# Attention beside an MLP on one core: four numbers of the schedule changed (first load of the output projection, pace of the MLP, split of a weight piece, release of raw weights)

## The chip, the cores and the metric

The kernel runs on one core of a Trainium2 chip. The metric is device time in microseconds (us), from the start to the end of one execution. The core has five engines that each run their own instructions in order: TensorE (PE; its weight loads are shown apart as PEld), VectorE (DVE), ScalarE (ACT), GpSimd (POOL) and SyncE (SP), which here only issues transfers. A line such as L580 is line 580 of the kernel before.

## The reference

All is float32, with 2048 tokens, 576 channels, 32 heads of 18 channels and an MLP with 4608 hidden channels:

```
g = sigmoid((x * gate_w).sum(-1, keepdims=True))
qkv = (x @ wqkv).reshape(1, 2048, 3, 32, 18)
p = softmax(einsum("bhqd,bhkd->bhqk", q, k) * 18 ** -0.5)
a = einsum("bhqk,bhkd->bhqd", p, v) -> (1, 2048, 576) @ wo
b = gelu(layernorm(x) @ w1 + b1) @ w2 + b2
return g * a + (1 - g) * b
```

The softmax is over all 2048 keys, and gelu is the tanh form.

## The kernel before

**Numbers.** To keep float32 accuracy with the matrix engine's rounded format (fp32r), an operand is held as a rounded part (hi) and the rest (lo), and a product is made of three matmuls: hi by hi, hi by lo and lo by hi. A split is thus a copy (hi) and a subtraction (lo).

**Start.** x is transposed on TensorE (L768). The weights wqkv come in seven column pieces, cut by W_CUT; `split_w` makes hi on ScalarE (L762) and lo on VectorE or POOL (L763). Pieces 0 and 1 are split in two parts, the chunks 0 to 2 and the chunks 3 and 4 of the 576 input channels; the later pieces in one. q and k are the matmuls at L892, L894 and L895, v those at L913 to L916. This phase ends at about 228 us.

**Loop.** The attention is a loop of 512 steps: 32 units (a unit is two heads over half of the tokens) by 16 key blocks. In a step TensorE computes scores for the row maxima of a later unit (L229, reduced by VectorE at L231), scores for the exponential (L272, taken by ScalarE at L275), and, every two or three steps (`span`), a burst of products of the probabilities with v (L290). At the end of a unit's maxima VectorE finishes them (L239 to L242), TensorE transposes them (L246), ScalarE copies the rows (L248), and two transfers (L138) put them behind the queries; they go on POOL's queue or on SP's, depending on how long ago the last large load was. The sums and products of a finished unit are copied by VectorE (L301) and stored (L304, L310).

In the gaps between these matmuls the MLP's run: a generator gives them out piece by piece. A hidden tile is 54 matmuls at L492 (`h_pair`), followed by an activation chain on ScalarE (L513, L545, L543) and POOL (L182), which gives the split result hh and hl. An output tile is 48 matmuls at L580 (`out_pair`), added up by VectorE (L597) out of two accumulators. The pieces of a hidden tile are spread over one or two groups of gaps; what decides is how much work has been given out, against a pace:

```
behind[0] = base + (TOTAL - base) * step / FIN
...
elif (last and spent[0] >= behind[0]) or left < GAPS:
    left += GAPS
```

So FIN is the step at which the pace has all the MLP's work done. The MLP's weights are loaded raw and split once (ScalarE L396, POOL L182), stored, and loaded again for later token blocks. `LOADED` holds the slot from which a raw weight may be taken up: LAND (8) slots after its load was issued. Work that isn't TensorE's is queued (`bg`, `defer`) and handed out by slots.

**Output projection.** It is a generator too. `next(proj)` runs its first parts at the steps of PSTEP: at 489 the raw wo is loaded (L1059, L1057) and five splits are queued for POOL (L1052, L1053); at the second number `load_o(0)` and `load_den(0)` load a quarter of the attention's results (L1071, L1074) and its sums (L1096, L1099); at 495 seven stages of `normed(0, c)` are deferred (VectorE L1140 and L1150, ScalarE between) and two finished tiles of the MLP are loaded (L1128); at 497 the next quarter follows. The results are loaded into a tile of the pool that also held the raw wo. When the MLP is done and step 498 is past, the matmuls of the projection (L1227) take the MLP's place in the gaps; those left at the loop's end run behind it. VectorE mixes at L1231, and `out` is stored at L1238 or L1241. The MLP's finished output goes through memory: stored at L604, loaded at L1122.

Of the kernel before, what the change touches and what calls it, by code (L numbers as in the profile page):

```python
# [40 lines left out]
LAND = 8  # L41
# [7 lines left out]
PLAN = [[(), (0,), (1,), (2,), (3,), (4,), (5, 6), ()], [(), (0,), (1,), (2,), (3,), (4,), (5, 6), ()],  # L49
        [(), (), (), (0, 1), (2,), (3,), (4, 5), (6,)]]  # L50
LAST = 28
PSTEP = (489, 492, 495, 497)
ORDER = (0, 1, 3, 2)
ROUNDS = [lambda g: 0, lambda g: 2 * (g in (9, 10, 16)), lambda g: 2 * (g % 2 or g == 16),
          lambda g: 2 * (g in (4, 5, 6, 7, 8, 10, 12, 14))]
# [6 lines left out]
W_AT = {0: 1, 1: 2, 2: 3, 4: 4, 6: 5, 7: 6}  # L62
W_CUT = (0, 128, 416, 704, 992, 2 * D, 3 * D - 288, 3 * D)
NSTEP = 512
FIN = NSTEP - 12
TWOS = NSTEP - 2 * NT


# [1 line left out]
def gated_mix_kernel(ctx: ExitStack, tc: tile.TileContext, x, wqkv, wo, w1, b1, w2, b2, gate_w, out):  # L70
# [70 lines left out]
    slot = [0]  # L141
# [61 lines left out]
    def load_k(pair, c0=0, c1=S):  # L203
        ka = KA[pair % 2]
        for h in range(2):
            d0 = D + (2 * pair + h) * DH
            for i, part in enumerate((0, 1, 0)):
                r = 64 * h + i * DH
                dma_r(nc.sync, ka[r:r + DH, c0:c1], qk_scr[part, d0:d0 + DH, c0:c1])
# [120 lines left out]
    looped = [False]  # L330
# [9 lines left out]
    def mlp():  # L340
# [3 lines left out]
        n = len(seq)  # L344
# [17 lines left out]
        def raw2(c):  # L362
            return R2[min(c // 2, 1)][c % 2]
        LOADED = {}
# [12 lines left out]
        def load_w2(c):  # L377
            if (2, c) in LOADED or c >= NFC:
                return
            LOADED[2, c] = slot[0] + LAND  # L380
            nc.sync.dma_start(raw2(c), w2[c * P:(c + 1) * P, :])

        def rounded(dst, src):
# [47 lines left out]
        def prep_w2(i):  # L431
            for m in range(G // 2):
                q = i * (G // 2) + m
                for j in range(2):
                    c = 2 * (q % NQ0) + j
                    if q >= NQ0:
                        reload(W2, (q, j), wp2, [P, 2, D], w2_scr[c])
                        continue
                    split(W2, (q, j), wp2, [P, 2, D], (2, c), raw2(c), w2_scr[c],
                          lambda c: load_w2(c + 2))  # L440
# [190 lines left out]
        for late, fn, k in ((1, load_w2, 0), (1, load_w2, 1), (3, load_w1, 1), (4, load_w2, 2), (4, load_w2, 3)):  # L631
            defer(late, lambda fn=fn, k=k: fn(k))
# [82 lines left out]
    with ExitStack() as a:  # L715
# [41 lines left out]
        def split_w(n, eng):  # L757
            c0 = W_CUT[n] if W_CUT[n] < 2 * D else W_CUT[n] - 2 * D
            hi, lo = [w_[:, :, c0:c0 + W_CUT[n + 1] - W_CUT[n]] for w_ in (W_QK if W_CUT[n] < 2 * D else W_V)]
            raw = wraw.pop(n)  # L760
            for cs in (slice(0, 3), slice(3, 5)) if n < 2 else (slice(0, 5),):
                nc.scalar.activation(hi[:, cs], raw[:, cs], AF.Copy)  # L762
                eng.tensor_tensor(lo[:, cs], raw[:, cs], hi[:, cs].bitcast(F32), op=ALU.subtract)  # L763

# [178 lines left out]
        for c in range(5):  # L943
            x_chunk(0, c)
            if c == 2:
                split_w(0, nc.vector)
                load_w(2)
        b1r = sm.tile([NFC, P], F32, name="b1r", bufs=1)
        for tb in range(NB):
            work = [(qk_group, (tb, mt)) for mt in (range(9) if tb < 2 else (4, 0, 1, 2, 3, 5, 6, 7, 8))] + [(v_group, (tb, t, n)) for t in range(4) for n in range(2)]  # L950
            for g, (fn, args) in enumerate(work):
                if tb == 0:
                    if g in W_AT:
                        n = W_AT[g]
                        split_w(n, nc.gpsimd if 2 < n < 6 else nc.vector)
                        if n + 2 < 7:
                            load_w(n + 2)
                    if g == 10:
                        nc.sync.dma_start(b2b, bcast_rows(b2, D))
                        nc.sync.dma_start(b1r, b1.rearrange("(c p) -> c p", p=P))  # L960
# [9 lines left out]
                if tb + 1 < NB:  # L970
# [12 lines left out]
                    c = g - at["x"]  # L983
# [267 lines left out]
    def fill(step, gap):  # L1251

        if over[0] is None and not stream and kept[0] == NT and step > PSTEP[-1] + 1:
            stream.append(proj)
            over[0] = step
            spent[0] = since[0] = 0.0
        if over[0] is None:
            piece[0] = gap
            behind[0] = base + (TOTAL - base) * step / FIN
            if gap not in skip:  # L1260
# [17 lines left out]
    for u in range(NU):  # L1278
        for kc in range(NT):
# [10 lines left out]
            if NU - 5 <= u < NU - 3 and kc % 4 == 1 and 0 < step - 16 * (NU - 5) - 1 < 17:  # L1290

                kb = (step - 16 * (NU - 5) - 5) // 4
                load_k(NPAIR - 1, kb * TB, (kb + 1) * TB)
            if step in PSTEP:
                assert hidden[0] == NB - 1
# [51 lines left out]
```

## Time and profile before

| | |
|---|---|
| median of 3 runs | 2227.85 us (2227.79 to 2228.08) |
| the profiled execution | 2229.34 us, span 2227.6 us |
| granted TensorE clock, mean | 1.000 |
| busy: TensorE, weight loads, VectorE, ScalarE, POOL | 99%, 71%, 74%, 64%, 45% of the span |
| TensorE, matmuls: L492 (64 rows, the large group), L580 (hh and hl) | 569.4 us, 487.1 + 351.1 us |
| TensorE: L272, L229 | 460.4 us, 435.1 us |
| transfers | 329.23 MB, mean 148 GB/s |

The profile gives busy time by group of instructions, the waits of each engine with what ended them, and the chain of work that ended last. A timeline row shows start, length, engine, line, instruction and count, and in square brackets the idle time ahead of it with its releaser. A row of the chain shows start, length and the work.

### The profile page before, as it was taken

What the parts mean: (1) busy time and instruction counts of PE and PEld (TensorE: products, weight loads), DVE (VectorE), ACT (ScalarE), POOL (GpSimd) and SP (SyncE); (2) the same over time, 40 slices, a digit from 0 to 9 for tenths busy, and PEclk for the clock granted to TensorE, in tenths of its full rate; (3) what the DMA queues carried; (4) which work ended last, traced back from release to release, by engine and by line L of the source; (5) the groups of instructions that cost most, each with busy time, mean ns of one, the idle gap of its engine ahead of it and who ended that gap; (6) DMA issues with size and microseconds to landing.
All of it is one profiled execution on the core that took longest, in us unless ns stands there. A gap on an engine that the chain in (4) does not pass through costs nothing.

```text
span 2227.6 us, 51540 instructions
## 1 busy us (share of the span) xinstructions
PE 2209.8 (99%) x20528; PEld 1583.7 (71%) x20528; DVE 1648.6 (74%) x2888; ACT 1429.3 (64%) x2655; POOL 1003.5 (45%) x1001
## 2 busy tenths in 40 slices
PE   8999999999999999999999999999999999999999
PEld 7878666766667766777666776766776776777668
DVE  6675777777778778777777777777777777777734
ACT  4333777777776666666666666666665666666772
POOL 4321766666664444444444444444444444444710
PEclk9999999999999999999999999999999999999999
DMA  8867555444464533333354424232464323242264
GB/s 266 270 222 220 192 174 162 145 159 148 151 195 139 195 102 120 123 120 104 113 171 151 136 79 135 100 124 100 120 177 145 107 103 121 102 148 93 89 223 168
DMA packets 164119, 329.23 MB, mean 148 GB/s; under 512 B 56830, under 2 KB 84090, under 8 KB 153150
## 3 DMA queue, kind: packets, MB, share of 16 engines
q1 hardware_dynamic: 161782, 322.19, 44.6%
q8 instruction: 162, 2.65, 0.5%
q10 hardware_dynamic: 1968, 3.70, 0.5%
q14 instruction: 79, 0.65, 0.1%
q0 software_dynamic: 128, 0.03, 0.0%
HBM read 233.47 MB, written 96.17 MB: 148 GB/s over the span
## 4 chain that ended last, share of the span: by engine, by line
PE 92%; DVE 3%; DMA 1%; ACT 1%; issue 1%; POOL 1%; SPq 0%; ACTq 0%; DVEq 0%; POOLq 0%
PE ps L290 20%; PE ps L492 20%; PE ps L580 19%; PE ps L272 13%; PE ps L229 11%; PE ps L892 3%; PE ps L1227 2%; PE ps L913 2%; DVE m L231 1%; DMA x<-in_B_w_dram 1%; ACT zz L545 1%; POOL w L182 0%; PE ps L768 0%; DMA p<-in_A_wqkv_dram 0%; PE ps L895 0%
## 5 line engine op out<-in xcount | busy, mean ns | idle before, releaser
L231 DVE TENSOR_REDUCE m<-ps 128x1 f32<-128x512 f32 x2048 | 1312.4, 684 | 406.7 <-PE ps L229 387.8
L275 ACT ACTIVATE p<-ps 128x512 f32<-128x512 f32 x1048 | 566.9, 595 | 265.7 <-PE ps L272 259.5
L275 ACT ACTIVATE ring<-ps 128x512 f32<-128x512 f32 x1000 | 542.3, 596 | 292.1 <-PE ps L272 288.7
L492 PE MATMUL ps<-big,w 64*128 64x512 f32 x3708 | 569.4, 393 | 0.2 <-issue 0.2
L182 POOL TENSOR_SCALAR zz<-zz 128x512 f32<-128x512 f32 x288 | 178.3, 619 | 746.1 <-ACT zz L545 713.7
L580 PE MATMUL ps<-w,hh 64*128 64x288 f32 x4352 | 487.1, 294 | 1.0 <-DVE x L597 1.0
L272 PE MATMUL ps<-qa,ka 56*128 56x512 f32 x2048 | 460.4, 421 | 3.5 <-ACT p L275 1.7
L580 PEld LDWEIGHTS ps<-w,hh 64*128 64x128 f32 x4352 | 426.8, 186 | 28.9 <-DVE x L597 4.2
L229 PE MATMUL ps<-ka,qa 54*128 54x512 f32 x2048 | 435.1, 398 | 0.6
L492 PEld LDWEIGHTS ps<-big,w 64*128 64x128 f32 x3708 | 368.9, 187 | 68.2 <-issue 0.5
L182 POOL TENSOR_TENSOR zz<-zz,z 128x512 f32<-128x512 f32 x288 | 371.4, 1290 | 24.0
L272 PEld LDWEIGHTS ps<-qa,ka 56*128 56x128 f32 x2048 | 212.7, 184 | 209.2 <-DVE m L231 165.0
L580 PE MATMUL ps<-w,hl 64*128 64x288 f32 x2176 | 351.1, 292 | 0.8 <-POOL hl L182 0.8
L290 PE MATMUL ps<-p,vt 128*32 128x512 f32 x1968 | 239.2, 598 | 0.0
L229 PEld LDWEIGHTS ps<-ka,qa 54*128 54x128 f32 x2048 | 220.0, 185 | 25.1 <-DVE m L231 4.9
L580 PEld LDWEIGHTS ps<-w,hl 64*128 64x128 f32 x2176 | 234.7, 185 | 1.2 <-POOL hl L182 1.1
L290 PE MATMUL ps<-ring,vt 128*32 128x512 f32 x1872 | 227.6, 598 | 0.0
L182 POOL TENSOR_TENSOR hl<-zz,hh 128x512 fp32r<-128x512 f32 x136 | 176.7, 1299 | 11.3
L182 POOL TENSOR_TENSOR w<-x,w 128x576 fp32r<-128x576 f32 (+1 forms) x54 | 98.7, 1842 | 168.3 <-ACT w L396 147.9
L290 PEld LDWEIGHTS ps<-p,vt 128*32 128x32 f32 x1968 | 52.6, 109 | 111.9 <-issue 102.6
L290 PEld LDWEIGHTS ps<-ring,vt 128*32 128x32 f32 x1872 | 50.0, 109 | 106.3 <-issue 106.3
L597 DVE SCALAR_TENSOR_TENSOR x<-ps,x 128x288 f32<-128x288 f32 x256 | 104.1, 448 | 8.6 <-PE ps L580 8.6
(124 smaller groups left out, 1562.3 us busy)
## 6 DMA issues: line engine op xcount, KB each, us to landing
w<-w_scr SPq DMA_DIRECT2D x54, 1152.0 KB
w<-w_scr SPq DMA_DIRECT2D x108, 576.0 KB
x<-in_B_w_dram SPq DMA_DIRECT2D x72, 288.0 KB
w_scr<-w SPq DMA_DIRECT2D x18, 1152.0 KB
w_scr<-w SPq DMA_DIRECT2D x36, 576.0 KB
qa<-qk_scr SPq DMA_DIRECT2D x192, 72.0 KB
ka<-qk_scr SPq DMA_DIRECT2D x84, 144.0 KB
qk_scr<-hh SPq DMA_DIRECT2D x36, 256.0 KB
```

What stands on the lines that cost most here:

```text
L182: fn(*args, **kw)
L229: nc.tensor.matmul(ps, qa[r0:r0 + 54, t * P:(t + 1) * P], ka[r0:r0 + 54, kb * TB:(kb + 1) * TB], start=True, stop=True)
L231: nc.vector.tensor_reduce(M4[u][:, h, t, kb:kb + 1], ps, axis=AX.X, op=ALU.max)
L272: nc.tensor.matmul(ps[h], ka[r0:r0 + 56, kc * P:(kc + 1) * P], qa[r0:r0 + 56, qb * TB:(qb + 1) * TB], start=True, stop=True)
L275: nc.scalar.activation(p_of(n)[:, qb, h], ps[h], AF.Exp, scale=SCALE)
L290: nc.tensor.matmul(OB[u][r:r + 32, :], v[:, k, 19 * h:19 * h + 32], p_of(c)[:, qb, h, :], start=(k == 0), stop=(k == NT - 1))
L492: nc.tensor.matmul(ps[h], wt[w_][r, c, :], y[r, c, :], start=(k == 0), stop=(k == 26))
L580: mm = nc.tensor.matmul(ps[nn][:, :ND], h_[r, tok], w_[p_][r, cs[nn]], start=(k == 0), stop=(k == 6 * G - 1))
L597: nc.vector.scalar_tensor_tensor(dst, ps[nn][:, :ND], 0.5, b2b[:, cs[nn]] if g == 0 else dst, op0=ALU.mult, op1=ALU.add)
L892: nc.tensor.matmul(ps, w_[:, c, ms], big[:, s_, :], start=(k == 0), stop=False)
L913: nc.tensor.matmul(ps[:, :ND], big[:, s_, tok], w_[:, c, cs], start=(k == 0), stop=False)
L1227: nc.tensor.matmul(ps[:, :ND], OT[b][2][:, s_, tok], w_part(w_, c)[:, cs], start=(k == 0), stop=(k == 13))
```

## The change

Four numbers or conditions change.

```diff
-PSTEP = (489, 492, 495, 497)
+PSTEP = (489, 493, 495, 497)
...
-FIN = NSTEP - 12
+FIN = NSTEP - 10
...
         def load_w2(c):
             if (2, c) in LOADED or c >= NFC:
                 return
-            LOADED[2, c] = slot[0] + LAND
+            LOADED[2, c] = slot[0] + LAND + 2 * looped[0]
             nc.sync.dma_start(raw2(c), w2[c * P:(c + 1) * P, :])
...
-            for cs in (slice(0, 3), slice(3, 5)) if n < 2 else (slice(0, 5),):
+            for cs in (slice(0, 3), slice(3, 5)) if n < 3 else (slice(0, 5),):
                 nc.scalar.activation(hi[:, cs], raw[:, cs], AF.Copy)
                 eng.tensor_tensor(lo[:, cs], raw[:, cs], hi[:, cs].bitcast(F32), op=ALU.subtract)
```

The first load of the projection is issued in the program at step 493 instead of 492. The MLP's pace reaches its end at step 502 instead of 500. The third piece of wqkv (n = 2, W_CUT 416 to 704, 288 columns) is split in two parts as the first two are. In the loop (`looped[0]` is 1 there, 0 before) a raw second weight may be taken up ten slots after its load instead of eight.

The pace moves instructions on TensorE from about 1690 us on. The first place, in the 181st group of its order counted by the bursts of L290, stands for the pacing. Before, four times six L580 of an output tile, and a gap without MLP work between two pairs of score matmuls (the numbers behind names are tiles of the pools):

```order
L272 MATMUL ps<-qa_104,ka_107 128x512 x2
L580 MATMUL ps<-w_24781,hh 128x288 x4
L580 MATMUL ps<-w_24781,hl 128x288 x2
L229 MATMUL ps<-ka_107,qa_105 128x512 x2
L272 MATMUL ps<-qa_104,ka_107 128x512 x2
L229 MATMUL ps<-ka_107,qa_105 128x512 x2
L272 MATMUL ps<-qa_104,ka_107 128x512 x2
L580 MATMUL ps<-w_24779,hh 128x288 x4
L580 MATMUL ps<-w_24779,hl 128x288 x2
L229 MATMUL ps<-ka_107,qa_105 128x512 x2
L290 MATMUL ps<-p,vt_109 32x512 x8
```

Now, in the same group, the second half of a hidden tile cut in 14 pieces:

```order
L272 MATMUL ps<-qa_104,ka_107 128x512 x2
L492 MATMUL ps<-big,w_24299 128x512 x4
L229 MATMUL ps<-ka_107,qa_105 128x512 x2
L492 MATMUL ps<-big,w_24299 128x512 x4
L272 MATMUL ps<-qa_104,ka_107 128x512 x2
L492 MATMUL ps<-big,w_24299 128x512 x4
L229 MATMUL ps<-ka_107,qa_105 128x512 x2
```

The output tile's matmuls follow this hidden tile now, in groups of 48, where before three groups shared 144 of them unevenly.

The second place is on ScalarE, between the last activation of the MLP and the copy of the last maxima's rows (L248, which follows L246). Before:

```order
L513 ACTIVATE z<-ps,b1t 128x512
L545 ACTIVATE zz<-z 128x512 x2
L275 ACTIVATE p<-ps 128x512 x4
L543 ACTIVATE zz<-zz 128x512
L275 ACTIVATE p<-ps 128x512 x2
L275 ACTIVATE ring_2355<-ps 128x512 x2
L543 ACTIVATE zz<-zz 128x512
L275 ACTIVATE ring_2355<-ps 128x512 x2
L275 ACTIVATE p<-ps 128x512 x8
L275 ACTIVATE ring_2355<-ps 128x512 x4
L275 ACTIVATE p<-ps 128x512 x2
L248 ACTIVATE oe<-ps 32x128
```

Now:

```order
L513 ACTIVATE z<-ps,b1t 128x512
L545 ACTIVATE zz<-z 128x512 x2
L275 ACTIVATE ring_2357<-ps 128x512 x2
L275 ACTIVATE p<-ps 128x512 x2
L543 ACTIVATE zz<-zz 128x512
L275 ACTIVATE p<-ps 128x512 x4
L543 ACTIVATE zz<-zz 128x512
L275 ACTIVATE p<-ps 128x512 x2
L275 ACTIVATE ring_2357<-ps 128x512 x4
L275 ACTIVATE p<-ps 128x512 x2
L248 ACTIVATE oe<-ps 32x128
```

Between them stood 24 exponentials, now 16: eight fewer, which is one group of two key blocks. The MLP's last hidden tile is one group nearer to the copy.

The third place is SP's queue from the load of wo to the first loads for the projection. Before:

```order
L1059 DMA x<-in_A_wo_dram 128x4x576
L322 DMA ot_scr<-dn_scr 36x1x1024
L1057 DMA x<-in_A_wo_dram 64x576 x2
L1071 DMA x<-ot_scr 128x4x512
L1074 DMA x<-ot_scr 64x512 x2
L1096 DMA low<-ot_scr 128x4x512
L1099 DMA low<-ot_scr 64x512 x2
L604 DMA b_scr<-x 128x576
L304 DMA dn<-oe 128x1x16
```

Now:

```order
L1059 DMA x<-in_A_wo_dram 128x4x576
L322 DMA ot_scr<-dn_scr 36x1x1024
L1057 DMA x<-in_A_wo_dram 64x576 x2
L138 DMA qa_105<-oe 2x8x128 x2
L1071 DMA x<-ot_scr 128x4x512
L1074 DMA x<-ot_scr 64x512 x2
L1096 DMA low<-ot_scr 128x4x512
L1099 DMA low<-ot_scr 64x512 x2
L304 DMA dn<-oe 128x1x16
```

The two transfers of the maxima's rows stand ahead of the load now; before, they were on POOL's queue behind the splits of wo. The first store L604 went from directly behind the loads to behind L304 and L310. The splits of wo stand directly behind POOL's last L182 in both, and VectorE's order around the first L1140 is the same in both: L239 to L242, four L597, L1140, two L597, L301.

## The prediction

> **What bounds the kernel now.** I read the page first: engines, the summary of the chain, then TensorE's waits.
>
> ```profile
> PE 2209.8 (99%) x20528; PEld 1583.7 (71%) x20528; DVE 1648.6 (74%) x2888; ACT 1429.3 (64%) x2655; POOL 1003.5 (45%) x1001
> PE 92%; DVE 3%; DMA 1%; ACT 1%; issue 1%; POOL 1%; SPq 0%; ACTq 0%; DVEq 0%; POOLq 0%
> ...
> PE ps L768 <- DMA x<-in_A_x_dram: 5.1, 1, 5.1
> PE ps L580 <- DVE x L597: 1.0, 3, 0.3
> PE ps L892 <- DVE wqk L763: 0.8, 1, 0.8
> PE ps L580 <- POOL hl L182: 0.8, 1, 0.8
> PE ps L913 <- DVE wv L763: 0.2, 1, 0.2
> ```
>
> TensorE is busy for 2209.8 of 2227.6 us and makes 92% of the chain. Of the 17.8 us in which it is idle, 5.1 are the first load. (The columns are sum, count, mean.) So no edit can gain much by removing waits. The time moves if the matmuls are packed otherwise, or if TensorE comes to wait where it does not now. A change of 0.2%, 4.46 us, is about what a measurement of this kernel can tell from none.
>
> **The pace (FIN).** The instruction order of TensorE is the same up to 1690 us; from there the changed kernel lays the same MLP matmuls out otherwise. I count in groups, each ended by a burst of L290; a group's time is the distance between the ends of two bursts. The chain of waits gives one place of each kind:
>
> ```profile
> 888.37 2.71 PE ps L290 x24
> 901.11 2.71 PE ps L290 x24
> ...
> 1699.18 1.85 PE ps L290 x16
> 1723.79 1.85 PE ps L290 x16
> 1730.93 1.85 PE ps L290 x16
> 1742.11 2.71 PE ps L290 x24
> ```
>
> Three groups between 1701.03 and 1725.64, 24.61 us together, hold 144 L580, as much as three regular groups, but unevenly: the slots without MLP work wait for VectorE's maxima and the full ones are TensorE-bound. The regular group behind them takes 7.14 (1725.64 to 1732.78). The next, three key blocks with a whole hidden tile (L492) cut finely, takes 12.04; one of these that also holds a row transposition (L246) took 12.74 (891.08 to 903.82). The end of the loop:
>
> ```profile
> 2082.85 1.85 PE ps L290 x16
> 2093.08 1.85 PE ps L290 x16
> 2116.10 0.21 PE ps L246
> 2120.89 1.85 PE ps L290 x16
> 2123.18 1.60 PE ps L580 x24
> 2127.07 1.85 PE ps L290 x16
> 2129.36 2.04 PE ps L580 x21
> 2133.85 1.99 PE ps L290 x16
> 2140.17 1.85 PE ps L290 x16
> 2146.65 1.85 PE ps L290 x16
> 2179.42 25.01 PE ps L1227 x187
> ```
>
> A two-block group with a hidden tile takes 10.23 (2084.70 to 2094.93), a late L580 group 6.18 (2122.74 to 2128.92), one with 22 L1227 6.48 (2142.02 to 2148.50).
> Gone in the changed order: the three uneven groups (24.61), one 10.23, one such with L246 (10.23 + 0.21 = 10.44), one with 22 L1227 (6.48): 51.76. New: one of 12.04, one of 12.74, two regular ones (2 x 7.14), one late L580 group (6.18): 45.24. The 22 L1227 are done behind the loop instead: 22 x 25.01 / 187 = 2.94. Together 45.24 + 2.94 - 51.76 = **-3.58**. The other groups with L246 keep the neighbours they had, so their small waits are the same. Bounds: -2.5 if the 12.74 and the regular groups each come out some tenths longer, -4 if the uneven groups' work packs better still.
>
> **The first load (PSTEP), and what it meets.** Here I expect the loss. POOL splits the output weights (five pairs, L1052 and L1053) directly behind the last activation of the MLP, in both kernels. Its timeline, then the SP wait, SP's and VectorE's timelines:
>
> ```profile
> 2115.95 1.41 POOL L1053 TENSOR_TENSOR wlast<-x,big 128x576 fp32r<-128x576 f32 x1
> ...
> SPq L1071 <- POOL wlast L1053: 5.1, 1, 5.1
> ...
> 2117.39 0.37 SPq L1071 DMA_DIRECT2D x<-ot_scr  x1
> ...
> 2128.18 0.69 DVE L1140 TENSOR_TENSOR x<-x,low 128x512 f32<-128x512 f32 x1 [6.43 <-DMA b_scr<-x]
> 2128.80 0.81 DVE L597 SCALAR_TENSOR_TENSOR x<-ps,x 128x288 f32<-128x288 f32 x2
> ```
>
> L1071 loads into the buffer of the raw weights, so SP waits 5.1 us for POOL's last split, which ends at 2117.36. The load thus moves with the end of the MLP's hidden work, not with PSTEP; one key block later in the program changes nothing while POOL is later still. From issue to the first L1140 pass 2128.18 - 2117.39 = 10.79 us (the transfer named in the bracket is the last of several awaited; the tile loads issued just ahead of it must land too). VectorE runs in order: two L597 stand behind L1140, and TensorE's next L580 need the accumulators that they free. Before, this costs 0.72: the group with the 21 recorded L580 ran from 2128.92 to 2135.84, 6.92, against the 6.18 or so of its neighbours.
> Now the places. From the end of the last hidden group (2094.93) POOL's splits end 2117.36 - 2094.93 = 22.43 later. L246 comes 2116.10 - 2094.93 = 21.17 later before: three L580 groups lie between. In the changed order two lie there, so L246 comes 21.17 - 7.13 = 14.04 later (7.13 is the middle one, regular). What stands behind L246 up to L1140 on VectorE is the same: four L597. So L1140 comes 7.13 later against TensorE than before, and nothing covers it, since 0.72 were lost already: the wait is 0.72 + 7.13 = 7.85. Added: **+7.13**. Bounds: +5.6 if the load takes 9.3 us instead of 10.79, +8 if the transfers moved onto SP ahead of it slow it.
> SP is moved past too: the two row transfers (L138) that POOL's queue issued behind the splits now go on SP ahead of L1071. They wait for L248, 14.04 plus a few tenths behind the hidden group, well before 22.43, so cost nothing; on POOL they would have waited. The first store L604 falls behind L304 and L310 on SP; what it feeds is read groups later. The later loads shift with TensorE; the last bt load is a group earlier against the tail, which I price at -0.2 (0 to -0.4).
>
> **After the wait.** A TensorE that has stood still may come back slow. At the start it waited 5.05, and then:
>
> ```profile
> 5.05 2.90 PE ps L768 x12
> 46.48 0.44 PE ps L768 x4
> 9.37 3.34 PE L892 MATMUL ps<-big,wqk 128*128 128x512 f32 x12
> 13.01 2.96 PE L892 MATMUL ps<-big,wqk 128*128 128x512 f32 x12
> ```
>
> 242 ns for each of the first twelve transpositions against 110 later: 12 x 0.132 = 1.58; 0.38 more on the first twelve L892: 1.96, and some for the eight L768 between. I take **+2.2** behind a wait of 7.85, bounds 0 (the first transpositions were held up by their inputs, not by the array) and +2.9 (all twenty slow).
> [...]
>
> **The third weight piece.** TensorE's waits at the start, with ScalarE and VectorE at that place and for a piece already cut in two:
>
> ```profile
> 20.98 2.60 PE L892 MATMUL ps<-big,wqk 128*128 128x512 f32 x10 [0.81 <-DVE wqk L763]
> 17.82 1.41 ACT L762 ACTIVATE wqk<-p 128x1440 fp32r<-128x1440 f32 x1 [4.01 <-DMA p<-in_A_wqkv_dram]
> 19.26 1.66 DVE L763 TENSOR_TENSOR wqk<-p,wqk 128x1440 fp32r<-128x1440 f32 x1 [4.73 <-ACT wqk L762]
> 10.72 1.49 ACT L762 ACTIVATE wqk<-p 128x864 fp32r<-128x864 f32 x2
> 11.67 1.73 DVE L763 TENSOR_TENSOR wqk<-p,wqk 128x864 fp32r<-128x864 f32 x2
> ```
>
> In two, the first three of five chunks are copied by 17.82 + 0.85 = 18.7 and their rest is ready at about 19.7, ahead of TensorE at 20.2; the second follows by 20.8. The wait of 0.81 goes, at an extra 0.1 on each of the two engines. What is late next is the weights for v (L913, where TensorE already waits 0.2), so I keep **-0.5** (0 to -0.8).
>
> **The second raw weights.** Taking them up two slots later moves, in six places, a pair of POOL splits behind the first two activation products.
>
> ```profile
> 354.68 2.97 POOL L182 TENSOR_TENSOR w<-x,w 128x576 fp32r<-128x576 f32 x2 [0.23 <-ACT w L396]
> 364.44 1.29 POOL L182 TENSOR_TENSOR hl<-zz,hh 128x512 fp32r<-128x512 f32 x1
> ```
>
> The same 2.97 of POOL work stands before or behind 2 us of other work, and the last product ends when it did. TensorE lost 0.8 to hl in the whole run, so the cover is TensorE's queue of L580 of tiles ready earlier. **0**, bounds -0.8 (that wait goes) and +0.8 (one like it comes).
>
> **Sum.** -3.58 + 7.13 + 2.2 - 0.5 - 0.2 + 0 = **+5.05**. The profiled execution took 2229.34, of which 2227.6 is span: it gives 2234.4. It lies 1.49 over the median 2227.85, which gives **2232.9**.
>
> **The rivals.**
> - *The array keeps its pace.* The wait comes, but matmuls run at once at 110 ns a transposition: 2232.9 - 2.2 = 2230.7, within 0.2%. For it speaks that the twelve slow L768 may have waited for tiles of x; against it the slow L892 behind them. Chance 0.22. [...]
> - *The load is early enough, and the kernel is faster.* If VectorE's L1140 lay behind the L597 at run time, or the data came within 3 us of issue, the 0.72 goes too: -3.58 - 0.72 - 0.5 - 0.2 = -5.0, 2222.9. It decides when issue to landing falls from 10.79 to under 2.94 (10.79 - 7.85). The order and the load's size, some 2.6 MB by its shapes, speak against it: 0.08.
> - *More is late.* The wait also holds VectorE's copy L301 and L1140's follow-ups, and the second weights bring a wait of their own in some of six places: 0.8 there, up to 2.9 for the cold array, and 2 for the next load: 2232.9 + 0.8 + 0.7 + 2 = 2236.4. Chance 0.15.
> - That the edits do nothing is excluded by the order for FIN and the split; for PSTEP alone it is nearly my forecast.
>
> **How the numbers follow.** Forecast 0.55, the rivals 0.22, 0.08 and 0.15. The bounds of the terms put the forecast itself at 2230.5 to 2235: two thirds of it lie over 2232.31, where slower begins. Slower: 0.55 x 0.65 + 0.15 x 0.95 + 0.22 x 0.1 = 0.52. Faster, under 2223.39: 0.07, nearly all from the second rival. Same: the remaining 0.41. The range leaves out the second rival and the upper part of the third: 2229.0 to 2236.5.
>
> **What will show it.** In VectorE's timeline of the changed kernel L1140 starts 11 us behind L1071, and TensorE's waits have a row L580 <- DVE L597 of 7 to 8 us: if it is under 3, the second rival holds. The L580 behind it take more than 1.60 for 24: if not, the first. L1071 still waits for POOL's L1053. The uneven groups at 1700 are gone, 144 L580 in three groups of 7.14. The row L892 <- DVE wqk L763 of 0.8 is gone, and the hl row is no larger. The prediction is wrong if L1140 is not what TensorE waits for, or if a wait appears between 300 and 1690 us.

## The result and the profile after

The changed kernel takes 2232.52 us (median of 14 runs, 2231.84 to 2233.68), the kernel before 2227.91 (14 runs on the same chip): 4.61 us more, ratio 1.0019 with an interval of 1.0012 to 1.0025. That is 0.2% to within its uncertainty.

The profiled execution after took 2232.68 with a span of 2230.9. The profiled execution before was a long one, 1.43 over the median of these 14 runs, so the two spans differ by 3.3 only. They divide as follows, by the ends of the bursts of L290 in the two timelines: -0.6 up to the first burst, -0.9 from there to the 178th (about 1680 us), +2.4 from there to the end of the loop, +2.5 behind the loop. The page's line of engines, after:

```profile
PE 2208.0 (99%) x20528; PEld 1585.2 (71%) x20528; DVE 1651.5 (74%) x2889; ACT 1430.0 (64%) x2656; POOL 1002.0 (45%) x999
```

TensorE's waits, after (sum, count, longest; the third column of the prediction's rows is also the longest, not the mean):

```profile
PE ps L580 <- DVE x L597: 6.3, 3, 5.7
PE ps L768 <- DMA x<-in_A_x_dram: 5.1, 1, 5.1
PE ps L246 <- DVE nm L242: 2.4, 6, 0.6
...
PE ps L272 <- ACT ring L275: 0.5, 3, 0.2
PE ps L580 <- POOL hl L182: 0.8, 1, 0.8
```

A wait of 5.7 stands where the longest was 0.3, the row L892 <- DVE wqk L763 is gone, and the hl row is as it was. The place of the long wait, in the timelines of SP, VectorE and TensorE:

```profile
2116.74 0.37 SPq L1071 DMA_DIRECT2D x<-ot_scr  x1
...
2113.84 0.82 DVE L597 SCALAR_TENSOR_TENSOR x<-ps,x 128x288 f32<-128x288 f32 x2 [4.25 <-PE ps L580]
2126.83 0.69 DVE L1140 TENSOR_TENSOR x<-x,low 128x512 f32<-128x512 f32 x1 [12.18 <-DMA low<-ot_scr]
2127.44 0.82 DVE L597 SCALAR_TENSOR_TENSOR x<-ps,x 128x288 f32<-128x288 f32 x2
...
2121.77 0.50 PE L272 MATMUL ps<-qa,ka 56*128 56x512 f32 x2
2127.95 1.21 PE L580 MATMUL ps<-w,hh 64*128 64x288 f32 x4 [5.68 <-DVE x L597]
```

Behind it, the chain of waits:

```profile
2127.95 3.61 PE ps L580 x24
2136.76 1.60 PE ps L580 x23
```

VectorE stands 12.18 us in front of L1140 until the loads that start with L1071 have landed (the bracket names the last of them, that of the sums); L1140 starts 10.09 behind the issue of L1071. The L597 behind it comes at 2127.44, and TensorE, which needed its accumulator at 2122.27, starts at 2127.95. Then it is slow: 24 L580 in 3.61 where the next group takes 1.60. Windows of TensorE over this stretch (columns: length, busy time and count of PE, PEld, DVE, ACT, POOL, then granted clock, DMA share, GB/s):

```profile
2121.00:2127.00 6.00, 1.27 (x10) 0.19 (x2) 0.17 (x1) 0.05 (x1) 0.00 (x0) 0.91 0.83 269
2127.95:2129.95 2.00, 2.00 (x15) 1.92 (x17) 2.00 (x4) 1.21 (x3) 0.75 (x1) 0.50 0.03 8
2129.95:2131.95 2.00, 2.00 (x17) 2.00 (x17) 1.67 (x4) 0.27 (x1) 0.00 (x0) 0.50 0.34 77
2131.95:2133.95 2.00, 2.00 (x26) 2.00 (x24) 1.41 (x3) 2.00 (x5) 0.00 (x0) 0.79 0.84 249
2133.95:2135.95 2.00, 2.00 (x23) 0.71 (x21) 2.00 (x4) 2.00 (x5) 0.51 (x1) 1.00 0.57 199
```

The granted clock is 0.50 until 2132.8. The whole group took 14.49 (2121.84 to 2136.33) against the 6.18 of the next: 5.68 of wait and 2.63 of slow work.

### The profile page after: what moved, and what is told of

Read it like the earlier page. It is cut to its first block, busy times and chain, and to the rows that moved or that the text cites. A ratio compares the mean times of both kernels' runs of the same rounds, so it can differ in the third digit from the quotient of the medians.

```text
span 2230.9 us, 51554 instructions
## 1 busy us (share of the span) xinstructions
PE 2208.0 (99%) x20528; PEld 1585.2 (71%) x20528; DVE 1651.5 (74%) x2889; ACT 1430.0 (64%) x2656; POOL 1002.0 (45%) x999
## 4 chain that ended last, share of the span: by engine, by line
PE 91%; DVE 3%; DMA 2%; POOL 2%; ACT 1%; issue 1%; SPq 0%; DVEq 0%; POOLq 0%; ACTq 0%
PE ps L290 20%; PE ps L492 20%; PE ps L580 19%; PE ps L272 12%; PE ps L229 11%; PE ps L892 3%; PE ps L1227 3%; PE ps L913 2%; DVE m L231 1%; DMA p<-in_A_wqkv_dram 1%; POOL zz L182 1%; ACT zz L545 1%; DMA low<-ot_scr 0%; DVE nmh L240 0%; PE ps L768 0%
## 5 line engine op out<-in xcount | busy, mean ns | idle before, releaser
L275 ACT ACTIVATE p<-ps 128x512 f32<-128x512 f32 x1048 | 566.7, 595 | 265.4 <-PE ps L272 258.3
L275 ACT ACTIVATE ring<-ps 128x512 f32<-128x512 f32 x1000 | 542.5, 596 | 283.7 <-PE ps L272 280.6
L182 POOL TENSOR_SCALAR zz<-zz 128x512 f32<-128x512 f32 x288 | 178.2, 619 | 748.0 <-ACT zz L545 716.5
L580 PE MATMUL ps<-w,hh 64*128 64x288 f32 x4352 | 485.7, 294 | 6.3 <-DVE x L597 6.3
L272 PE MATMUL ps<-qa,ka 56*128 56x512 f32 x2048 | 458.8, 420 | 2.6 <-ACT p L275 1.5
L580 PEld LDWEIGHTS ps<-w,hh 64*128 64x128 f32 x4352 | 426.2, 187 | 34.0 <-DVE x L597 8.8
L182 POOL TENSOR_TENSOR zz<-zz,z 128x512 f32<-128x512 f32 x288 | 371.4, 1289 | 24.0
L272 PEld LDWEIGHTS ps<-qa,ka 56*128 56x128 f32 x2048 | 212.2, 184 | 205.0 <-DVE m L231 164.1
L580 PE MATMUL ps<-w,hl 64*128 64x288 f32 x2176 | 350.2, 292 | 0.8 <-POOL hl L182 0.8
L290 PE MATMUL ps<-p,vt 128*32 128x512 f32 x1968 | 240.0, 598 | 0.0
L580 PEld LDWEIGHTS ps<-w,hl 64*128 64x128 f32 x2176 | 233.7, 185 | 1.1 <-POOL hl L182 1.1
L290 PE MATMUL ps<-ring,vt 128*32 128x512 f32 x1872 | 227.4, 598 | 0.0
L182 POOL TENSOR_TENSOR hl<-zz,hh 128x512 fp32r<-128x512 f32 x136 | 176.7, 1300 | 11.4
L182 POOL TENSOR_TENSOR w<-x,w 128x576 fp32r<-128x576 f32 (+1 forms) x54 | 98.6, 1844 | 166.8 <-ACT w L396 146.1
L290 PEld LDWEIGHTS ps<-p,vt 128*32 128x32 f32 x1968 | 52.5, 109 | 112.6 <-issue 102.8
L290 PEld LDWEIGHTS ps<-ring,vt 128*32 128x32 f32 x1872 | 49.7, 109 | 106.7 <-issue 106.7
L597 DVE SCALAR_TENSOR_TENSOR x<-ps,x 128x288 f32<-128x288 f32 x256 | 104.1, 449 | 14.6 <-PE ps L580 14.4
```

The costliest lines, as they stand in the source:

```text
L182: fn(*args, **kw)
L272: nc.tensor.matmul(ps[h], ka[r0:r0 + 56, kc * P:(kc + 1) * P], qa[r0:r0 + 56, qb * TB:(qb + 1) * TB], start=True, stop=True)
L275: nc.scalar.activation(p_of(n)[:, qb, h], ps[h], AF.Exp, scale=SCALE)
L290: nc.tensor.matmul(OB[u][r:r + 32, :], v[:, k, 19 * h:19 * h + 32], p_of(c)[:, qb, h, :], start=(k == 0), stop=(k == NT - 1))
L580: mm = nc.tensor.matmul(ps[nn][:, :ND], h_[r, tok], w_[p_][r, cs[nn]], start=(k == 0), stop=(k == 6 * G - 1))
L597: nc.vector.scalar_tensor_tensor(dst, ps[nn][:, :ND], 0.5, b2b[:, cs[nn]] if g == 0 else dst, op0=ALU.mult, op1=ALU.add)
```

## The experiments

The kernel before was timed beside each set; its median was 2228.86 in the first, 2228.85 in the second and 2228.53 in the third, so ratios are compared and not medians across sets. Each ratio is to the kernel before.

| kernel | median us | ratio, interval |
|---|---|---|
| late8 | 2228.24 | 0.9997, 0.9988 to 1.0006 |
| fin_only | 2232.39 | 1.0016, 1.0007 to 1.0025 |
| act_hi | 2229.51 | 1.0003, 0.9994 to 1.0011 |
| split_more | 2235.42 | 1.0026, 1.0015 to 1.0038 |
| split_only | 2227.27 | 0.9994, 0.9985 to 1.0002 |
| w2_only | 2227.49 | 0.9993, 0.9985 to 1.0002 |
| pstep_only | 2229.23 | 1.0002, 0.9993 to 1.0011 |
| before_late8 | 2229.29 | 1.0002, 0.9993 to 1.0010 |
| late16 | 2225.16 | 0.9984, 0.9976 to 0.9993 |
| after_again | 2232.65 | 1.0017, 1.0008 to 1.0025 |
| no_fin | 2227.45 | 0.9994, 0.9985 to 1.0003 |
| no_pstep | 2231.27 | 1.0010, 1.0001 to 1.0019 |

Small effects are therefore read from the traces: from the first burst of L290 to the 178th, some 1451 us, executions with the same edits there agree within 0.8 us, and most single groups within 0.05.

**Taking the load's wait from in front of L597 (late8).** The changed kernel with

```diff
-            defer(4 + 2 * c, lambda c=c: normed(0, c))
+            defer(8 + 2 * c, lambda c=c: normed(0, c))
```

> The changed kernel with the seven stages of normed(0, c) deferred by 8 + 2c slots in place of 4 + 2c, so that on VectorE the first L1140 stands behind six L597 instead of four. Theory (L1140, waiting for the late load, blocks L597, TensorE stands 5.7 us and then runs at half clock, 2.6 us): both go, 2232.5 - 8.3 = 2224.2, and no row L580 <- DVE L597 over 0.3. Rival (the load is late for whoever needs it, so the wait only moves): a wait of 3 us or more at L1227 or at a later L597, 2228 to 2232.

Half of it came. The L597 wait is gone and the clock stays at 1.00, but the group still takes 9.68 and the one behind it 6.85. TensorE's waits near the end, then ScalarE's:

```profile
PE ps L290 <- ACT ring L275: 2.0, 1, 2.0
...
ACT big L1143 <- DVE x L1140: 3.5, 1, 3.5
```

The rival had a point: L1140 no longer blocks VectorE's L597, but ScalarE's first L1143 waits for L1140, and exponentials that TensorE needs stand behind it in ScalarE's order. The wait moved to another engine and shrank.

**Moving it behind those exponentials too (late16).** The changed kernel with `defer(16 + 2 * c, ...)`.

> The changed kernel with normed(0, c) deferred by 16 + 2c slots: on VectorE L1140 behind two more L597 than in late8, and on ScalarE the first L1143 behind the exponentials of the group that waited in late8. Theory (in late8 the wait moved to ScalarE, where L1143 waits for L1140 ahead of exponentials; with both moved behind, nobody waits for the load): the 2.0 at L290 <- ACT L275 and the 1.5 of the pushed exponentials go, 4.1 + 3.5 less than the changed kernel on the same chip, so about 3.0 to 3.7 faster than the kernel before, ratio 0.9984 to 0.9987. Rival (the projection's first matmuls need the normed rows now): a wait of over 1 us at L1227, no faster than late8.

It takes 2225.16, ratio 0.9984, the lower bound of what was expected and faster than both kernels. TensorE's waits from 1670 us to the end:

```profile
PE ps L246 <- DVE nm L242: 1.0, 2, 0.7
PE ps L1227 <- DVE big L1152: 0.2, 1, 0.2
PE ps L272 <- ACT p L275: 0.2, 1, 0.2
PE ps L272 <- ACT ring L275: 0.2, 1, 0.2
```

The group that took 14.49 takes 6.20. Two of the next take 6.38 and 6.85, since ScalarE's copies still push exponentials. So the load was too late only for those who stood behind it in a queue: nobody needed it yet. From the 178th burst to the loop's end it takes 494.16 against 499.03 before, which is what the pace gains in the loop; behind the loop 2.5 of it are given back, as in the changed kernel.

**Which edit makes the wait (fin_only, pstep_only, no_pstep, no_fin, after_again).** Of the four edits only the pace, only PSTEP, and the changed kernel without each of these:

```diff
-FIN = NSTEP - 12
+FIN = NSTEP - 10
```

> The kernel before with FIN = NSTEP - 10 alone. Theory (the loss comes with the pace: the last hidden tile is a group nearer to the loads that wait for POOL's splits): all but the 0.6 that the split third piece gained at the start, so 2232.5 + 0.6 = 2233.1, with the wait of about 5.7 at L580. Rival (the loss comes with the later PSTEP): no such wait, and only the packing's gain, 2227.9 - 3.6 - 0.7 = 2223.6.

```diff
-PSTEP = (489, 492, 495, 497)
+PSTEP = (489, 493, 495, 497)
```

> The kernel before with PSTEP = (489, 493, 495, 497), nothing else. Theory (SP waits for POOL's last split in both, so the load is issued at the same time; only the two row transfers go on SP): 2227.9, and L1071 issued at 2117.4 as before. Rival (the later first load makes the wait): a wait of some us at L580 <- DVE L597, 2231 or more.

> The changed kernel with PSTEP = (489, 492, 495, 497) as before. Theory (as in fin_only: the row transfers go behind POOL's splits, TensorE waits 3.3 for them at L272 and about 0.9 at L580 in place of 5.7 at L580, and half clock follows; the groups from the rows' transposition on took 26.95 there against 28.03): 1.1 faster than the changed kernel on the same chip. Rival (PSTEP is what made the wait at L580): 6 or more faster than the changed kernel.

> The changed kernel with FIN = NSTEP - 12 as before. Theory (split and second weights gain 0.9 each by the ends of their phases in the profiles, PSTEP adds 0.3 at L580, and all that is lost comes with FIN): 1.5 faster than the kernel before, ratio 0.9993. Rival (the gains of the small edits are taken up later): ratio 1.0000.

> The changed kernel once more, so that the others stand beside it on one chip: 4.6 over the kernel before, ratio 1.0020.

The pace alone loses what the change loses, PSTEP alone nothing that can be measured. pstep_only issues L1071 at 2117.48 (before 2117.39), but counted from the end of the last hidden group that is 23.30 against 22.46, so 0.8 later: POOL's last split ended at 2116.63, and SP was still busy with the two row transfers ahead of the load, from 2115.89 to 2117.30. The theory's "issued at the same time" was thus wrong. It costs little: the group behind L1140 takes 7.21 against 6.91. But fin_only doesn't lose it in the way that was expected. TensorE's waits there:

```profile
PE ps L272 <- DMA qa<-oe: 3.3, 2, 1.8
...
PE ps L580 <- DVE x L597: 0.9, 1, 0.9
```

And POOL's timeline:

```profile
2117.41 1.43 POOL L1053 TENSOR_TENSOR wlast<-x,big 128x576 fp32r<-128x576 f32 x1
2118.78 1.17 POOL L138 DMA_DIRECT2D qa<-oe  x2
```

With PSTEP at 492 the rows of the last maxima stay on POOL's queue behind the splits, are issued at 2118.78, and TensorE waits for them at the first L272 of the last unit, 3.3 in two pieces. While it waits the load comes nearer, so 0.9 are left at L580. The expectation of no change in mechanism was wrong; in time the two ways cost nearly the same: the three groups from the rows' transposition on take 26.95 in fin_only and 28.03 in the changed kernel. no_pstep repeats the wait at L272 with 3.4, but has none at L580 near the end (0.9 expected); it is 1.4 us faster than after_again on the same chip (1.1 expected). no_fin stays at 0.9994 with no wait over 0.3 in the tail: the two small gains remain, and all the loss is the pace's.

**What sets the wait, and what comes behind it (act_hi, split_more).** In the changed kernel ScalarE makes the rounded copies of the output weights; and, the other way, POOL makes the last split twice (the result is the same):

```diff
-            nc.gpsimd.tensor_scalar(w_part(0, c), src, 1.0, 1.0, op0=ALU.mult, op1=ALU.mult)
+            nc.scalar.activation(w_part(0, c), src, AF.Copy)
...
+        bg.append((lambda: 0, lambda: split(4), SLOT, 0))
```

> The changed kernel with the five rounded copies of the output weights (L1052) made by ScalarE instead of POOL: POOL's splits end 5 x 0.69 = 3.4 us earlier, and so do the load and L1140. Theory (the idle time is set by POOL's splits, and half clock comes only behind an idle time of some length between 2.3 and 5.7): idle 5.7 - 3.4 = 2.3, clock stays at 1.00 behind it, 2232.5 - 3.4 - 2.6 = 2226.5, up to 1 more for ScalarE's 3.3 us of copies among the exponentials. Rival (the loss behind the wait is in proportion to it): 2.6 x 2.3 / 5.7 = 1.0 of loss stays, 2227.6, and the clock falls. Second rival (the wait isn't set by POOL): no change, 2232.5.

> The changed kernel with the last of the five splits of the output weights done twice on POOL (2.1 us more in front of L1071). Theory (POOL's end sets the wait one for one; the cost of the clock behind it is fixed): idle 5.7 + 2.1 = 7.8, then 2.6 as before, 2232.5 + 2.1 = 2234.6. Rival (the loss behind is in proportion): 2.6 x 7.8 / 5.7 = 3.6, 2235.6. Second rival (the wait isn't set by POOL): 2232.5.

TensorE's timeline at the wait and windows behind it, columns as above, first of act_hi:

```profile
2127.01 0.89 PE L580 MATMUL ps<-w,hh 64*128 64x288 f32 x4 [1.71 <-DVE x L597]
```

```profile
2126.00:2128.00 2.00, 0.99 (x9) 0.81 (x11) 2.00 (x5) 1.38 (x3) 0.58 (x1) 0.94 0.00 0
2128.00:2130.00 2.00, 2.00 (x20) 2.00 (x20) 2.00 (x4) 0.22 (x1) 0.17 (x1) 0.50 0.14 31
2130.00:2132.00 2.00, 2.00 (x24) 2.00 (x21) 1.59 (x4) 1.58 (x4) 0.00 (x0) 0.70 0.55 173
```

Then of split_more:

```profile
2129.57 1.21 PE L580 MATMUL ps<-w,hh 64*128 64x288 f32 x4 [8.26 <-DVE x L597]
```

```profile
2124.00:2126.00 2.00, 0.00 (x0) 0.00 (x0) 0.00 (x0) 0.00 (x0) 0.00 (x0) 0.82 1.01 379
2132.00:2134.00 2.00, 2.00 (x16) 2.00 (x16) 1.28 (x4) 0.70 (x2) 0.00 (x0) 0.50 0.36 89
2134.00:2136.00 2.00, 2.00 (x22) 2.00 (x20) 1.80 (x3) 2.00 (x5) 0.00 (x0) 0.62 0.97 310
```

split_more shows that POOL's end sets the wait: with 2.1 more work in front of the load it is 8.26 (7.8 expected). act_hi shows less than its 1.71 (2.3 expected) suggests. ScalarE's and SP's timelines there:

```profile
2112.19 0.69 ACT L1052 ACTIVATE big<-x 128x576 fp32r<-128x576 f32 x1 [3.22 <-DMA x<-in_A_wo_dram]
2114.01 1.40 SPq L138 DMA_DIRECT2D qa<-oe  x2
2115.59 0.37 SPq L1071 DMA_DIRECT2D x<-ot_scr  x1
```

POOL's last split ended at 2114.36, counted from the last hidden group 3.5 earlier than in the changed kernel. But ScalarE stood 3.22 in front of its last copy until the raw wo had landed, with exponentials and L248 behind that copy. So the rows were late, their transfers held SP until 2115.41, and L1071 was issued only 2.3 earlier. Mainly for the same reason the group with L246 takes 9.26 instead of 7.35, and TensorE came 1.9 later to the place where it waits. The two together, less 0.2 for a slower load, make the wait 4.0 shorter; that this lies near the 3.4 of the theory is luck. The expectation that a short wait leaves the clock alone fell: behind 1.71 us it goes to 0.50, and that group takes 10.03, or 2.1 more than wait and work. So 2226.5 was missed by 2 to 3. In split_more the group takes 17.54: 8.26 of wait, 6.18 of work, 3.1 of slow work. Its ratio times 2227.91 is 2233.7, with an interval of 2231.3 to 2236.4 that holds the fixed cost (2234.6) and the proportional one (2235.6). The slow work behind the wait is neither: 2.1 behind 1.71 us in act_hi, 2.63 behind 5.68 in the changed kernel, 3.1 behind 8.26 here.

**The small edits alone (split_only, w2_only).** They are the parts of the diff shown above.

> The kernel before with the third weight piece split in two parts, nothing else. Theory (the wait of 0.8 at L892 goes, the start ends 0.6 earlier, and nothing takes it up): 2227.9 - 0.6 = 2227.3. Rival (VectorE bounds the start anyway): 2227.9.

> The kernel before with the second raw weights taken up two slots later, nothing else. Theory (POOL's last product ends when it did, the gain of 0.9 between 320 and 700 us in the profiles is a difference between executions): 2227.9. Rival (the 0.9 is a gain of this edit): 2227.0.

Both ratios hold 1 within their intervals. In the traces both gains show. The first burst of L290 ends at 226.52 in split_only and at 227.95 before; over the profiled executions with the split (nine) and without it (five) that end varies by 1.7 and 0.8, and the means, 227.1 and 227.9, lie 0.8 apart. From that burst to the 178th, nine executions with the later second weights take 1450.85 to 1451.67, five without them 1452.02 to 1452.55: the means differ by 1.0, so the rival was right. The place, ScalarE's timeline around 410 us, before and then w2_only:

```profile
408.58 0.68 ACT L396 ACTIVATE w<-x 128x576 fp32r<-128x576 f32 x1 [0.83 <-DMA x<-in_B_w_dram]
409.17 1.06 ACT L275 ACTIVATE ring<-ps 128x512 f32<-128x512 f32 x2
410.69 0.68 ACT L396 ACTIVATE w<-x 128x576 fp32r<-128x576 f32 x1 [0.45 <-DMA x<-in_B_w_dram]
```

```profile
408.70 1.09 ACT L275 ACTIVATE p<-ps 128x512 f32<-128x512 f32 x2 [0.23 <-PE ps L272]
409.67 0.63 ACT L543 ACTIVATE zz<-zz 128x512 f32<-128x512 f32 x1
410.19 1.26 ACT L396 ACTIVATE w<-x 128x576 fp32r<-128x576 f32 x2
```

Before, ScalarE took the raw weights up before they had landed, stood 0.83 and 0.45 waiting for the transfer, and held up exponentials; that group took 8.35 and takes 6.98. In four like places 7.40 became 6.98. Three other groups lost 0.6 to 0.9 each, which gives part of it back.

**The same deferral in the kernel before (before_late8).**

> The kernel before with normed(0, c) deferred by 8 + 2c slots, nothing else. Theory (the small waits behind L1140 go, and nothing else): 2227.9 - 0.7 = 2227.2, so that beside late8 the pace and the split are worth about 3. Rival (a later L1140 delays the projection's first matmuls): 2228.5 or more.

Nothing was won, though not as the rival says: the projection's first matmuls are no slower (6.50 against 6.49 for their first group). The group behind L1140 falls from 6.91 to 6.17, but the next rises from 6.19 to 6.84, where ScalarE's copies for the projection stand ahead of exponentials. The 0.7 moved; what the deferral wins beside the later pace is the wait that the pace made. The kernel before with the deferral of late16 was not run.

## Why the prediction was right, and where it was not

- **The forecast's chain** held at each link. L1071 was issued when POOL's last split ended (2116.74; POOL ends 22.46 behind the last hidden group, 22.43 taken), L1140 came behind the load, L597 behind L1140, TensorE behind L597, and it came back slow. fin_only, no_fin and late16 show that the pace makes this, and that its removal gives it back. 2232.9 was forecast, 2232.52 measured; +5.05 against +4.61.
- **The pace, -3.58.** Up to L246 the counted groups give 39.06 - 45.28 = -6.22; measured -6.28 (429.43 against 435.71). Behind it two things were not foreseen, 0.7 each. L246 waits 0.6 for the rounding of the maxima, shown below, and the last burst of L290 takes 0.7 longer, because two copies for the projection stand ahead of the last exponentials on ScalarE:

```profile
2177.08 0.65 ACT L1146 ACTIVATE hh<-x 128x512 fp32r<-128x512 f32 x1
2177.60 0.63 ACT L1147 ACTIVATE big<-x 64x512 fp32r<-64x512 f32 x1
2178.12 1.07 ACT L275 ACTIVATE p<-ps 128x512 f32<-128x512 f32 x2
```

  The work behind the loop grew by 2.47, where 2.94 - 0.2 was taken.
- **The wait, 7.85, was mis-sized: 5.68.** The step that failed is the one by which "nothing covers it, since 0.72 were lost already". The 0.72 before were only in small part a late start of the L580: their first stood 0.38 behind the burst ahead of it (2129.30 against 2128.92), where the groups on both sides have 0.27. So about 0.6 of the 0.72 were no wait at this place. L1140 came 10.09 behind the load's issue, not 10.79, and L246's group was 0.7 longer.
- **After the wait, +2.2: 2.63 measured**, with the clock at 0.50. TensorE worked from 2127.95 to 2132.81 at that clock, and half of these 4.86 us is 2.43; in act_hi and split_more the same working gives 1.7 and 3.0, against 2.1 and 3.1 measured. The rival that the array keeps its pace is out.
- **The second raw weights, 0: about -1.0 measured.** The step looked at POOL, whose work moved but cost nothing, and overlooked the other instruction that the release moves, ScalarE's L396, which was waiting for its transfer in front of exponentials. The row of TensorE's waits that shows it, L272 <- ACT ring L275 (1.4 before with a longest of 0.9, now 0.5 and 0.2), was not read.
- **The third weight piece, -0.5:** the wait went, and 0.6 (the profiled pair) to 0.8 (the means) is what the traces show.
- **PSTEP** was priced as nothing but a harmless move of two transfers. With the earlier pace the move holds the load back by 0.8 (pstep_only). With the later pace that move is not free of effect: without it TensorE waits for the rows themselves (fin_only, no_pstep). It exchanges one wait for another that costs 1.1 to 1.4 more.
- **The range and chances.** The measured difference lies at the bound of 0.2%, between "same" and "slower". The total came out nearer than its parts. On the profiled execution the sum gave 2234.4, and the one after took 2232.68, 1.7 less: +0.7 twice in the pace, -2.2 for the wait, +0.4 for the slow work, -0.9 for the second weights, -0.3 behind the loop and -0.1 at the start make -1.7. The medians differ by less because the profiled execution before lay 1.43 over its median and the one after 0.16, so that the forecast took off 1.49 for a difference of which 0.16 was left after; part of the closeness is luck.

## What to carry to other kernels

A late transfer costs by what is queued behind the instruction that waits for it, on each engine in turn: find that instruction, then its readers on other engines, and move all of them behind the work that is due; here this turned a loss of 0.17% into a gain of 0.16%, with the transfer as late as ever (0.06% of that gain are there without the pace, in no_fin). When an edit moves instructions, list every engine's instructions that it moves and look up each in the waits, also those that the edit wasn't about. A wait of TensorE has to be priced with the slow time behind it, which here was 2.1 to 3.1 us behind single waits of 1.7 to 8.3, and nothing behind one of 2.0.

## What the runs showed of the hardware that was not expected

**How long the clock stays low.** In windows of 0.1 us the granted clock is 0.50 from 2125.98 to 2132.81 in the changed kernel (6.83 us; 6.83 in after_again too), from 2127.77 to 2131.19 in act_hi (3.41), from 2125.31 to 2128.72 in fin_only (3.41), from 2121.54 to 2128.36 in no_pstep (6.83), and from 2125.26 to 2135.51 in split_more (10.24): one, two or three times 3.41. The changed kernel's clock falls once more behind the last matmul, at 2231.79, which is 98.99 or 29 times 3.413 behind the rise at 2132.81. Why these stretches have such lengths is not shown.

In act_hi the clock fell with an idle stretch of 1.71 us, 0.76 us after work had resumed, while in late8 it stayed at 1.00 with one of 1.97 us (2127.31 to 2129.28). So in these traces the length of the idle stretch alone doesn't tell whether the clock falls. Nor was there one delay: from the start of the idle stretch to the fall passed 2.47 us in act_hi, 3.71 in the changed kernel, 3.95 in split_more and 5.18 in after_again, and from the return of work to the rise 4.18, 4.86, 5.94 and 6.22. What else counts, the runs don't show.

**At the start** the first transpositions are slow, and the window view still gives 1.00 for the clock there. But the trace's record of the clock begins only at 10.04 us in the kernel before, and the view counts time without a record as 1.00. The transpositions (L768) up to 9.36 us and from 10.05 to 60 us in the kernel before, shortest, median and longest in ns:

```profile
L768 PE MATMUL ps<-ident,x x20: 417/419/477, 5.1 to 9.3; 128*128 128x128 f32 x20
L768 PE MATMUL ps<-ident,x x36: 269/272/273, 46.3 to 58.3; 128*128 128x128 f32 x36
```

The change comes where the record begins. In the kernel before the L892 that starts at 9.37 took 774 ns, the one at 9.94 took 440, and the ten behind them 389 to 399. In the changed kernel, whose record begins at 9.71, the one at 9.43 took 619 and the eleven behind it 392 to 398. So the rows from which the price of the slow time was taken show matmuls that were slow themselves, and not a wait for x; what the clock was in that stretch is not recorded.

**A small VectorE copy beside POOL.** The rounding of the last maxima (L240, 128 x 16) took 0.47 before and 1.16 after. VectorE and POOL, after, then VectorE before:

```profile
2106.99 1.16 DVE L240 CAST nmh<-nm 128x16 fp32r<-128x16 f32 x1
2106.71 1.42 POOL L1053 TENSOR_TENSOR big<-x,big 128x576 fp32r<-128x576 f32 x1
```

```profile
2114.79 0.47 DVE L240 CAST nmh<-nm 128x16 fp32r<-128x16 f32 x1
```

After, it began 0.28 behind a POOL subtraction and ended with it, at 2108.15 and 2108.13. Before, the subtraction it met ran from 2113.81 to 2115.23, and the copy ended at 2115.26. The other places settle what this is. The copy runs once in each of the 32 units, so the traces before and after hold 64 of it. The 30 that met no POOL instruction under way took 0.17 to 0.18, so that the 0.47 was also held up. 34 began while a subtraction, product or copy of POOL ran, and none of them ended before it: 22 were stretched and ended 0.03 to 0.04 behind POOL's instruction, the other 12 began in its last 0.11 us, took 0.17 to 0.18 and ended 0.07 to 0.13 behind it. What the two share is not shown.
